# A fixed order table in place of a list scheduler, with convolution taps spread over three engines, in a windowed attention and gated feed-forward kernel

## The chip, the cores and the metric

The kernel runs on one core of one Trainium2 chip. The metric is the device time of one execution in microseconds (us). Executions scatter by one or two per cent, so a kernel is judged by the median of several runs, always beside runs of the kernel before on the same chip. Every ratio here is the mean time of one kernel's fast runs over that of the other kernel's fast runs of the same rounds, so it is not quite the ratio of the medians that are quoted with it. A difference between two variants in us, where it says "by the ratios", is the difference of their two ratios times the median of the kernel before (about 235 us). A run counts as slow when it lies more than 1.5% above the fastest run of its kernel, and as fast otherwise. The *granted clock* is the share of TensorE's full clock that the chip allowed.

Engine names in profile lines: PE is TensorE, PEld its weight loads, DVE is VectorE, ACT is ScalarE, POOL is GpSimd, SPq is the queue of the engine that issues most transfers. A trailing q means an engine's sequencer, and "issue" is time in which nothing that the profile shows was waited for.

## The reference

Attention over a band of 32 positions to each side, then a feed-forward layer with a three-tap convolution along the sequence and a gate:

```python
B, H, S, D = 8, 8, 576, 64          # d_model 512, d_ff 1024
scores = q @ k.T / sqrt(D);  mask = abs(i - j) <= 32
attn   = softmax(where(mask, scores, -1e9)) @ v
x      = attn.transpose(0, 2, 1, 3).reshape(B, S, H * D)
h      = maximum(x @ w_in, 0.0)
conv_out = sum(conv_w[k] * h_padded[:, k:k + S, :] for k in range(3))
gate   = 1.0 / (1.0 + exp(-conv_out))
out    = (h * gate) @ w_out
```

## The kernel before

The sequence of all batches is cut into twelve chunks of 384 positions, numbered 0 to 11. Attention of a pair of batches makes the input of three chunks. A *unit* is one chunk times 128 of the 1024 hidden columns (there are 96, eight of them in two halves). Its convolution runs on TensorE, one matmul with a diagonal matrix for each tap. In most units the middle tap is done by VectorE, which adds `h * w` onto the sum in PSUM:

```python
on_dve = m < P["tap"][c]              # tap: (0, 0, 8, 8, 8, 8, 8, 8, 7, 8, 8, 8)
kks = (0, 2) if on_dve else (0, 1, 2)
def emit_pc(e_):
    for kk in kks:
        tensor.matmul(pc.ap[:, 0:nc_], diag_w[:, kk, m, :], taps(kk), start=(kk == 0), stop=(kk == 2))
...
if on_dve:
    def emit_tap(e_):
        vector.scalar_tensor_tensor(
            out=in3(pc.ap), in0=taps(1), scalar=conv_w_sb[:, 1, m:m + 1], in1=in3(pc.ap),
            op0=ALU.mult, op1=ALU.add)
```

The relu stands on ScalarE, the diagonals, the masks and the "shifts" (copies of v moved by 64 partitions) on VectorE. GpSimd only casts. No order is written down: each operation carries costs, a priority and a list of engines, and a list scheduler simulates the engines and takes the ready operation of lowest priority:

```python
'e_vo': (('DVE',), ('DVE',), ('DVE',)),      # engines for the shifts
'mask': ('DVE',),
...
op(f"pc {u}", {"PE": len(kks) * (nc_ / 2400.0 + 0.0025)}, emit_pc, prio + 0.5, ...)
order = pl.run(P["start"], (0.107, "filler", P["thin"]), P["fill"], pf)
for t, _, e, o in order:
    o.emit(e)                                 # or a filler: a matmul on a tile of zeros
```

The softmax here doesn't subtract the row's maximum and nothing guards it: scores larger than these inputs give would overflow.

Of the kernel before, what the change touches and what calls it, by code (L numbers as in the profile page):

```python
# [9 lines left out]
FP32 = mybir.dt.float32  # L11
# [5 lines left out]
class Pool:  # L17


    def __init__(self, bufs):  # L20
        self.bufs = bufs
        self.free = [(-1.0, i) for i in range(len(bufs))]


    def take(self, span):

        if not self.free:
            return None
        self.free.sort()
        return self.free.pop(0)[1]  # L30

    def room(self, spans, spare):
        return len(self.free) >= len(spans) + spare

    def give(self, now, index, span):
        self.free.append((now, index))

    def ap(self, index, span):
        return self.bufs[index]


class Banks:


    def __init__(self, tile_):
        self.tile = tile_
        self.free = {i: -1.0 for i in range(8)}

    def runs(self, span):
        return [i for i in range(9 - span) if all(i + k in self.free for k in range(span))]  # L50

    def take(self, span):
        if span == 1:
            at = min(self.free, key=lambda i: (i < 3, self.free[i], -i))
        else:
            at = self.runs(span)[0]
        for k in range(span):
            del self.free[at + k]
        return at

    def room(self, spans, spare):
        if len(self.free) < sum(spans) + spare:
            return False
        return all(s == 1 or self.runs(s) for s in spans)

    def give(self, now, index, span):
        for k in range(span):
            self.free[index + k] = now

    def ap(self, index, span):  # L70
        return self.tile[:, 512 * index:512 * (index + span)]


class Slot:


    def __init__(self, pool, span=1):
        self.pool, self.span, self.index, self.users = pool, span, None, 0

    @property  # L80
    def ap(self):
        return self.pool.ap(self.index, self.span)


class Op:
    def __init__(self, name, cost, emit, prio, acquire, spare, mode, two):
        self.name, self.cost, self.emit, self.prio = name, cost, emit, prio
        self.acquire, self.spare, self.mode, self.two = acquire, spare, mode, two
        self.uses, self.after, self.follow, self.left = [], [], [], 0
        self.ready = 0.0  # L90


class Planner:



    LATENCY = {"PE": 0.05, "ACT": 0.045, "DVE": 0.045, "POOL": 0.075, "SP": 0.075}
    switch = 0.1

    def __init__(self):  # L100
        self.ops = []
        self.writer, self.readers = {}, {}
        self.fillers = None

    def op(self, name, cost, emit, prio, reads=(), writes=(), reserve=(), acquire=(), use=(),
           spare=0, mode=None, two=False, behind=None, early=0.0):
        o = Op(name, cost, emit, prio, list(acquire), spare, mode, two)
        o.early = early
        before = set()
        for k in reads:  # L110
            if k in self.writer:
                before |= self.writer[k]
        for k in list(writes) + list(reserve):
            before |= self.readers.get(k, set()) | self.writer.get(k, set())
        for k in reads:
            self.readers.setdefault(k, set()).add(o)
        for k in writes:
            self.writer[k], self.readers[k] = {o}, set()
        before.discard(o)
        o.left = len(before) + (behind is not None)  # L120
        if behind is not None:
            behind.follow.append(o)
        for p in before:
            p.after.append(o)
        o.uses = list(acquire) + [s for s in use if s not in acquire]
        for s in o.uses:
            s.users += 1
        self.ops.append(o)
        return o

    def run(self, start, filler, filler_until, late):

        engines = ("SP", "PE", "POOL", "ACT", "DVE")
        free = dict(start)
        todo = {e: [] for e in engines}
        events, out = [], []
        mode = None
        lock = {"DVE": 0.0, "POOL": 0.0, "PE": 0.0}
        dma_free, rings = 0.0, []
        gone = set()  # L140
        number = {o: i for i, o in enumerate(self.ops)}
        heap, count = [], 0

        def push(t, kind, x):
            nonlocal count
            count += 1
            heapq.heappush(heap, (t, count, kind, x))

        def offer(o):
            for e in o.cost:  # L150
                todo[e].append(o)
                todo[e].sort(key=lambda x: (x.prio, number[x]))


        busy, warm, win = {}, False, -1

        def rate(t):
            nonlocal warm, win
            w = int((t - 1.9) // 3.413)
            while win < w:  # L160
                b = busy.get(win, 0.0) / 3.413
                warm = (b > 0.35) if warm else (b > 0.85)
                win += 1
            return 1.0 if warm else 2.0

        def note(t, d):
            while d > 1e-9:
                w = int((t - 1.9) // 3.413)
                x = min(d, 1.9 + (w + 1) * 3.413 - t)
                busy[w] = busy.get(w, 0.0) + max(x, 1e-6)  # L170
                t, d = t + max(x, 1e-6), d - max(x, 1e-6)

        late.take(1)
        push(filler_until, "free", late)
        for o in self.ops:
            if not o.left:
                push(o.early, "ready", o)
        for e in engines:
            push(free[e], "look", e)
        left = len(self.ops)  # L180
        now = 0.0
        while left or heap:
            if not heap:
                raise RuntimeError("stuck: " + str([(o.name, o.left) for o in self.ops if o not in gone][:40]))
            now, _, kind, x = heapq.heappop(heap)
            batch = [(kind, x)]
            while heap and heap[0][0] <= now + 1e-9:
                _, _, kind, x = heapq.heappop(heap)
                batch.append((kind, x))
            for kind, x in batch:  # L190
                if kind == "ready":
                    offer(x)
                elif kind == "free":
                    x.give(now, 7, 1)
                elif kind == "done":
                    for s in x.uses:
                        s.users -= 1
                        if not s.users:
                            s.pool.give(now, s.index, s.span)
                    for n in x.after:  # L200
                        n.left -= 1
                        if not n.left:
                            push(max(now, n.early), "ready", n)
            if heap and heap[0][0] <= now + 1e-9:
                push(now, "look", None)
                continue
            for e in engines:
                while free[e] <= now + 1e-9:
                    best, blocked = None, False
                    other = {"DVE": "POOL", "POOL": "DVE"}.get(e, "PE")  # L210
                    for o in todo[e]:
                        if o in gone:
                            continue
                        if o.two and lock[other] > now + 1e-9:
                            blocked = True
                            continue
                        need = {}
                        for s in o.acquire:
                            need.setdefault(s.pool, []).append(s.span)
                        if not all(p.room(n, o.spare if p is self.psum else 0) for p, n in need.items()):  # L220
                            continue
                        key = o.prio + (self.switch if e == "PE" and o.mode != mode else 0.0)
                        if best is None or key < best[0]:
                            best = (key, o)
                        if e != "PE":
                            break
                    todo[e] = [o for o in todo[e] if o not in gone]
                    if best is None:
                        if blocked:
                            free[e] = lock[other]  # L230
# [795 lines left out]
```

## Time and profile before

| what | before |
|---|---|
| time, median of 3 runs | 236.68 us (235.42 to 236.8) |
| span of the profiled run | 234.2 us |
| first feed-forward matmul | 24.63 us |
| last matmul of the attention | 187.1 us |
| TensorE's last work | 229.7 us |
| GpSimd | 27% busy, nothing after 158 us |

The three instants in the table cut the span into a ramp, a middle in which attention and feed-forward overlap, and a tail in which only feed-forward is left. The windows view gives for each stretch its length, then the busy time (and number) of PE, PEld, DVE, ACT and POOL, the granted clock of TensorE, the busy share of the DMA engines (which the view can show above 1.00) and GB/s:

```profile
0.00:24.63 24.63, 18.57 (x305) 12.69 (x306) 18.52 (x62) 16.72 (x42) 11.21 (x41) 1.00 0.99 297
24.63:187.10 162.47, 158.69 (x2258) 93.64 (x2257) 149.40 (x346) 139.08 (x335) 51.59 (x61) 1.00 0.82 211
187.10:229.70 42.60, 42.56 (x232) 22.19 (x228) 29.07 (x58) 25.16 (x55) 0.00 (x0) 1.00 0.21 68
```

TensorE fills the tail to the last tenth of a microsecond, VectorE two thirds of it, GpSimd none. The groups to be compared later, with busy time and mean ns of one after the bar:

```profile
L380 DVE SCALAR_TENSOR_TENSOR pf<-hT,conv_w_sb,pf 128x384 f32<-128x384 bf16 x79 | 46.0, 616 | 11.4 <-PE pf L380 10.3 <-ACT attn L380 0.4
L380 PE MATMUL pf<-hT,diag_w 128*128 128x384 bf16 x185 | 40.7, 327 | 0.3 <-DVE diag_w L380 0.2
L380 DVE TENSOR_TENSOR attn<-attn,mask 128x1152 bf16<-128x1152 bf16 x32 | 27.5, 859 | 5.2 <-ACT attn L380 4.8
```

The first is the VectorE tap, the second the tap on TensorE, the third the mask.

### The profile page before, as it was taken

The numbers are of one execution on the slowest core, as the hardware profiler recorded it, in microseconds if no ns is written. First come the engines' busy times: TensorE is split into PE (matmuls) and PEld (weight loads), VectorE is DVE, ScalarE is ACT, GpSimd is POOL, SyncE is SP. The second block draws the span as 40 slices with busy tenths as digits, with TensorE's granted clock in tenths as the row PEclk, the third lists the DMA queues.
The fourth block names the chain that finished last, engine by engine and source line by source line (L and its number), as shares of the span: only waits on it lengthen the run. The fifth ranks groups of instructions, "written<-read, shape, count | busy, mean of one in ns | idle before, by whom it ended". The sixth has DMA issues, their size and how long they took to land.

```text
span 234.2 us, 7175 instructions
## 1 busy us (share of the span) xinstructions
PE 219.8 (94%) x2790; PEld 128.5 (55%) x2790; DVE 197.5 (84%) x463; ACT 181.6 (78%) x432; POOL 62.8 (27%) x101
## 2 busy tenths in 40 slices
PE   7777999899999899999999999999999999999992
PEld 4555556578555555655555555555555655555550
DVE  6489989896999999999999999887997995867271
ACT  3796989999999697798689687797599855766361
POOL 4336655552733531152360210340000000000000
PEclk9999999999999999999999999999999999999999
DMA  6999999999999988649995994981442143211204
GB/s 219 294 261 393 284 264 299 359 201 379 201 321 326 243 273 242 153 55 264 372 196 60 253 186 119 328 219 46 69 75 99 48 88 102 92 45 45 91 3 179
DMA packets 66054, 45.37 MB, mean 194 GB/s; under 512 B 51148, under 2 KB 51172, under 8 KB 66020
## 3 DMA queue, kind: packets, MB, share of 16 engines
q1 hardware_dynamic: 65984, 44.90, 71.1%
q8 instruction: 22, 0.36, 0.8%
q14 instruction: 12, 0.10, 0.1%
q10 hardware_dynamic: 36, 0.01, 0.0%
HBM read 32.52 MB, written 9.44 MB: 179 GB/s over the span
## 4 chain that ended last, share of the span: by engine, by line
PE 65%; DVE 19%; ACT 5%; DMA 3%; issue 3%; SPq 1%; ACTq 0%; POOL 0%; DVEq 0%; POOLq 0%
PE pf L380 65%; DVE gT L380 5%; DVE attn L380 4%; DMA vst<-in_v_dram 3%; DVE pf L380 3%; DVE diag_w L380 3%; ACT attn L380 2%; DVE vo L380 2%; DVE xn L380 1%; SPq L380 1%; ACT pf L380 1%; ACT xn L380 1%; DVE rec L380 1%; DVE qkT L380 1%; DVE xT L380 1%
## 5 line engine op out<-in xcount | busy, mean ns | idle before, releaser
L380 PE MATMUL pf<-xT,w_in_sb 128*128 128x385 bf16 (+2 forms) x416 | 73.9, 315 | 1.4 <-DVE gT L380 0.9
L380 PE MATMUL pf<-w_out_sb,gT 128*128 128x512 bf16 x288 | 67.8, 379 | 0.1
L380 ACT ACTIVATE pf<-pf 128x384 f32<-128x384 f32 (+1 forms) x104 | 47.0, 478 | 13.1 <-DVE pf L380 12.3
L380 ACT ACTIVATE hT<-pf 128x385 bf16<-128x385 f32 (+2 forms) x104 | 48.1, 501 | 11.3 <-PE pf L380 10.1
L380 DVE SCALAR_TENSOR_TENSOR gT<-pf,hT 128x384 bf16<-128x384 f32 (+1 forms) x104 | 51.4, 519 | 5.9 <-ACT pf L380 5.3
L380 DVE SCALAR_TENSOR_TENSOR pf<-hT,conv_w_sb,pf 128x384 f32<-128x384 bf16 x79 | 46.0, 616 | 11.4 <-PE pf L380 10.3
L380 PEld LDWEIGHTS <-w_in_sb 128*128 128x128 bf16 x416 | 38.8, 98 | 24.9 <-issue 2.7
L380 PE MATMUL pf<-hT,diag_w 128*128 128x384 bf16 (+1 forms) x233 | 46.3, 310 | 0.7 <-DVE gT L380 0.3
L380 POOL TENSOR_SCALAR qkb<-st 128x1152 bf16<-128x1152 f32 (+1 forms) x27 | 29.6, 1097 | 57.2 <-DMA st<-in_q_dram 30.5
L380 PEld LDWEIGHTS <-gT 128*128 128x128 bf16 x288 | 27.4, 98 | 29.7 <-ACT attn L380 0.3
L380 ACT ACTIVATE attn<-pf 128x512 bf16<-128x512 f32 (+1 forms) x96 | 41.0, 528 | 2.1 <-PE pf L380 1.9
L380 POOL TENSOR_SCALAR ve<-vst 128x512 bf16<-128x512 f32 x37 | 25.0, 682 | 30.4 <-DMA vst<-in_v_dram 24.6
L380 DVE TENSOR_TENSOR attn<-attn,mask 128x1152 bf16<-128x1152 bf16 x32 | 27.5, 859 | 5.2 <-ACT attn L380 4.8
L380 ACT COPY y<-pf 128x512 f32<-128x512 f32 x32 | 19.5, 612 | 11.1 <-PE pf L380 7.4
L380 PEld LDWEIGHTS <-diag_w 128*128 128x128 bf16 x233 | 19.8, 97 | 13.2 <-issue 0.8
L380 ACT COPY qkT<-pf 128x576 bf16<-128x576 bf16 x36 | 22.7, 660 | 1.8 <-PE pf L380 1.7
L380 DVE TENSOR_TENSOR xn<-pf,rec 128x256 bf16<-128x256 f32 x64 | 23.4, 408 | 0.1
L380 DVE COPY qkT<-pf 128x576 bf16<-128x576 bf16 x28 | 20.4, 748 | 2.9 <-PE pf L380 2.3
L380 DVE COPY vo<-ve 64x520 bf16<-64x520 bf16 (+1 forms) x28 | 15.4, 549 | 2.0 <-POOL ve L380 1.2
L380 PEld LDWEIGHTS <-attn 128*64 128x64 bf16 x576 | 11.8, 110 | 9.4 <-issue 5.7
L380 PE MATMUL pf<-ve,attn 128*64 128x65 bf16 x320 | 15.0, 197 | 2.1 <-DVE attn L380 1.2
L380 PE MATMUL pf<-qkT 64*128 64x64 bf16 x576 | 14.3, 191 | 1.6 <-DVE qkT L380 0.9
(39 smaller groups left out, 139.4 us busy)
## 6 DMA issues: line engine op xcount, KB each, us to landing
st<-in_q_dram SPq DMA_DIRECT2D x16, 576.0 KB, 6.7
st<-in_k_dram SPq DMA_DIRECT2D x16, 576.0 KB, 7.2
out_dram<-y SPq DMA_DIRECT2D x36, 256.0 KB, 2.4
vst<-in_v_dram SPq DMA_DIRECT2D x24, 256.0 KB, 8.5
vst<-in_v_dram SPq DMA_DIRECT2D x16, 192.0 KB, 7.5
st<-in_moe_w_in_dram SPq DMA_DIRECT2D x2, 1024.0 KB, 7.1
st<-in_moe_w_out_dram SPq DMA_DIRECT2D x2, 1024.0 KB, 7.8
xT<-xn SPq DMA_TRANSPOSE x30, 2.5
```

The costliest lines, as they stand in the source:

```text
L380: return lambda *args, **kwargs: fixed(do(*args, **kwargs))
```

## The change

The intent: give GpSimd, idle for most of the span, part of the convolution, so that TensorE has fewer diagonal matmuls; move other work so that no engine is overfull at one time; and write the result down as one searched order instead of leaving it to a greedy list. The core of the diff:

```diff
-class Planner:
-    ... (the list scheduler, its costs, priorities and engine lists)
-P = {'start': ..., 'st': 4, 'attn': 4, 'gT': 2, 'y': 4, ...}
+BUFS = {'st': 3, 'qkb': 5, 'qkT': 3, 'attn': 2, 'rec': 4, 'xn': 3, 'hT0': 8, 'hT1': 6, 'hT2': 6, 'cp': 2, 'gT': 4, 'y': 7}
+CONV = (            # one letter per unit, one row per chunk
+    '33333333',
+    '33q3323r23223321',
+    's222r32q',
... (chunks 3 to 7)
+    'qq23q1q2',
+    'r3rqrq23',
+    '12qrrq1q',
+    '2rrr2rrq',
+)
+ORDER = """
+15D 11D0 12D 1F 17D 2F 13D1 2F 14D 7F 28G 0V 1P0 2F 2V 33V 1F 4G 4F 20G0 21S 2F 16D 5G 1F 22S1 41P120 42P 23S 3G
... (40 more lines: operation number, engine letter, buffers; F is so many fillers)
+    TAPS = {         # taps on TensorE, on GpSimd, on VectorE
+        "3": ((0, 1, 2), (), ()), "2": ((0, 2), (), (1,)), "1": ((0,), (), (1, 2)),
+        "q": ((), (0, 2), (1,)), "r": ((), (0,), (1, 2)), "s": ((0,), (1, 2), ()),
+    }
... (in the unit)
+            def emit_times(e_, cp, kk):
+                gpsimd.tensor_scalar(
+                    out=in3(cp.ap), in0=taps(kk), scalar1=w_tap(kk), scalar2=0.0, op0=ALU.mult, op1=ALU.add
+                )
+            def emit_add(e_, cps=cps):
+                gpsimd.tensor_tensor(out=in3(cps[0].ap), in0=in3(cps[0].ap), in1=in3(cps[1].ap), op=ALU.add)
```

Engine letters: P, V, S, G for the four compute engines, D and Q for transfers issued by the sync engine and by ScalarE. A "q" unit has no matmul: GpSimd makes two products and their sum, and VectorE adds its tap and writes PSUM. The order also puts 24 diagonals and 6 masks on GpSimd, 28 relus on VectorE, and 11 of the long shifts on DMA queues.

## The prediction

> **What bounds the kernel now.** I read the busy shares first, then their course over the span, then the chain that ended last, and only then single groups. Columns of the first fence: busy time, share of the span, instructions; then the same in 40 slices.
>
> ```profile
> PE 219.8 (94%) x2790; PEld 128.5 (55%) x2790; DVE 197.5 (84%) x463; ACT 181.6 (78%) x432; POOL 62.8 (27%) x101
> ...
> PE   7777999899999899999999999999999999999992
> ...
> DVE  6489989896999999999999999887997995867271
> ACT  3796989999999697798689687797599855766361
> POOL 4336655552733531152360210340000000000000
> ```
>
> No engine is free all along: TensorE and VectorE are both at nine tenths in the middle, and in the last fifth VectorE and ScalarE fall off while GpSimd does nothing. So the work is badly spread in time, not only over engines. The windows (columns PE, weight loads, VectorE, ScalarE, GpSimd) give sizes: before the first feed-forward matmul, then up to the end of attention, then the tail.
>
> ```profile
> 0.00:24.60 24.60, 18.57 (x305) 12.69 (x306) 18.49 (x62) 16.69 (x42) 11.18 (x41) 1.00 0.99 297
> 24.60:190.00 165.40, 161.59 (x2275) 95.41 (x2275) 152.33 (x355) 139.97 (x337) 51.62 (x61) 1.00 0.81 208
> 190.00:229.70 39.70, 39.66 (x212) 20.42 (x209) 26.17 (x48) 24.30 (x54) 0.00 (x0) 1.00 0.21 70
> ```
>
> VectorE is 26.2 of 39.7 us busy in the tail: 13.5 us that the middle could have used. The chain says which engine sets the end where:
>
> ```profile
> PE 65%; DVE 19%; ACT 5%; DMA 3%; issue 3%; SPq 1%; ACTq 0%; POOL 0%; DVEq 0%; POOLq 0%
> ...
> 24.21 5.16 DVE diag_w L380 x15
> 29.37 0.48 DVE gT L380
> ...
> 161.90 67.35 PE pf L380 x589
> ```
>
> The last 67 us are TensorE alone. VectorE's 19% lies in the ramp and the middle, and 5.16 us of it is the building of diagonals, one block just when the first chunk starts.
>
> The busy time of PE overlaps itself: eight output matmuls of 379 ns each run from 200.80 to 202.53 in the timeline, 0.216 us apart. I therefore use start-to-start spacings: output matmul 0.216, input matmul of 385 columns 0.166, diagonal matmul 0.163 (384) or 0.083 (192), 18 transposes 0.315, 18 scores 0.35, 8 value matmuls 0.157. Times the counts this is 196.5 us of TensorE, without fillers. On VectorE, back to back in the chain, a tap takes 0.53 us and a gate 0.46.
>
> One more thing decides the risk, the same multiplication by the mask, once beside a GpSimd cast and once without:
>
> ```profile
> 74.36 1.47 DVE L380 TENSOR_TENSOR attn<-attn,mask 128x1152 bf16<-128x1152 bf16 x1
> ...
> 89.89 0.74 DVE L380 TENSOR_TENSOR attn<-attn,mask 128x1152 bf16<-128x1152 bf16 x1
> ...
> 74.08 1.15 POOL L380 TENSOR_SCALAR qkb<-st 128x1152 bf16<-128x1152 f32 x1 [1.87 <-DMA st<-in_q_dram]
> ```
>
> It took 0.74 us with GpSimd idle and 1.47 us when a cast had started 0.28 us earlier.
>
> **What the Trainium skill says.** "SBUF — State Buffer", section "Who interferes with whom": GpSimd and VectorE share one port pair; a VectorE instruction with two SBUF inputs waits for a GpSimd one that reads SBUF, and whichever started first keeps the pair for its whole instruction; an instruction with at most one SBUF input and no two-port mode is free of it. The trace agrees (the two masks). "GPSIMD Engine Reference", section "Performance versus the Vector engine": a two-input operation there costs about 2.6 cycles an element, 4497 ns for 2048 floats against 2293 on VectorE. No two-input operation runs on GpSimd in the kernel before, so its trace cannot say. "Perfetto Trace Analysis", section "Optimizing Scalar/DVE Operations", says that offloading between VectorE and GpSimd might not help, for the same port; section "Optimization Strategy", that interleaving regimes with different busiest engines can. The change does both.
>
> **The change part by part.** Counts come from comparing the instruction lists of both kernels per engine.
>
> TensorE: diagonal matmuls of 384 columns go from 185 to 118, of 192 from 48 to 35: 67 x 0.163 + 13 x 0.083 = 12.0 us less. Four more transposes of xn cost 0.3. Need: 196.5 to 184.8 us.
>
> VectorE loses 24 diagonals (x 0.24 = 5.8), 12 long and 6 short value shifts, most of them now DMAs (12 x 0.70 + 6 x 0.29 = 10.1), 26 taps onto PSUM (13.8), 6 masks (6 x 0.73 = 4.4), 16 normalisations (x 0.33 = 5.3): 39.4 us. It gains 33 long and 2 short taps that add a GpSimd product (18.1 at the price of a tap, an estimate), 8 short taps (2.6), 4 sums (2.0), 28 relus (23 x 0.47 + 5 x 0.27 = 12.2, priced by the slope of the xT casts), 7 copies of qkT (4.6), 10 casts (3.5), 2 copies of y (1.2): 44.2. Net +5 us: VectorE is not relieved at all, it is only filled more evenly.
>
> ScalarE: 28 relus fewer (-10.7), 7 qkT and 2 y copies fewer (-4.9); 64 more normalising activations (64 x 0.22 = 14.1), 9 casts of v (4.7), a few other casts (4.2). Net +7 us.
>
> GpSimd: casts of 128x512 at 0.62 and 128x1152 at 1.15 give 0.83 ns an element plus 0.2. So 60 products of 384 at 0.51 and 3 short ones (31.7), 24 diagonals at 0.30 (7.2), 7 shifts (5.7); by the skill's two-input rate 24 sums at about 1.0 (24) and 6 masks at 2.7 (16), both estimates; fewer casts -16. Net +69: 62.8 becomes about 130 us.
>
> To see what this does to the end I cut each order at the first matmul group of each of the twelve chunks and summed each engine's spacings in each piece; the largest sum is the least that piece can take. After the ramp these largest sums add up to 195.2 us before and 184.4 after. In reality those pieces of the kernel before took 229.7 - 24.6 = 205.1 us, 9.9 more than the sum. The gain lies at the end: pieces 8 to 11 need 61.9 us of TensorE against 45.0 of VectorE before, 55.9 against 52.8 after. Attention is not moved much later; it is taps that leave TensorE in the chunks where VectorE and GpSimd were idle.
>
> Sum: ramp 24.6 + 184.4 + the same loss 9.9 + 4.5 from TensorE's end to the end of the span + 2.5 by which the timed 236.68 exceeds the span of 234.2 = 225.9 us. Three corrections. The ramp: first FFN still needs all of batch 0, VectorE loses the diagonals and its shifts, but ScalarE's work before that point grows from 17.1 to 19.3 and a v load goes ahead of the first q; I take -2. The port: +4 (next part). A fixed order for all engines, evidently searched for, should lose less than a greedy list: -4. I predict 224 us, 5% less.
>
> **The rivals.** First, VectorE becomes the bound through the shared port. Masks (26), the 35 taps with two SBUF inputs, casts and shifts on VectorE are some 80 instructions that can be held. GpSimd would be busy 57% of the time with operations of 0.5 to 2.7 us, whose mean remainder I work out as 0.49 us: 80 x 0.57 x 0.49 = 22 us, of which the 32 masks before already paid about 4 (mean 859 ns, free 730). If all 18 us lay on the path the time would be 238 us, no gain. For it: the two masks above, and VectorE's 98% in the windows of the middle. Against it: in the pieces after the ramp TensorE and ScalarE are as large as VectorE, so much of a wait is taken up, and the old scheduler already kept such operations apart, so the new order surely does.
>
> Second, TensorE's relief is fully used and the order is nearly free of waits: ramp 22 + 184.4 + 3 + 7 = 216 us. For it: the 67 us tail shows TensorE can run without a gap when fed. Against it: three engines within 3 us of each other in sum (184.8, 187, 185) cannot all be without gaps in fixed order.
>
> Third, data: staging buffers go from 4 to 3, attention buffers from 4 to 2, and some 2.9 MB of shifts join the DMA queues, whose engines show nine tenths in the first 18 slices. If loads arrive later, fixed orders stall everything behind a late cast: 230 us or more. Against it: loads stand at nearly the same place of the order as before, and GpSimd waited 55 us for q and v without harm to TensorE, whose waits for GpSimd's qkb sum to 1.7 us.
>
> **Range and chances.** The rivals give 216, 230 and 238 around 224; the first and third can partly come together with the second's gain. I take 214 to 233 for 8 in 10. The 2% line is 232.0 us, near the upper end. Chances: 0.83 faster, 0.13 within 2%, 0.04 slower.
>
> **What would show it.** In the changed kernel's page: GpSimd near 130 us and busy to the end; VectorE about 200 to 210 us but now over 90% of the span; TensorE's tail no longer one stretch of 67 us in the chain, with VectorE's share of the chain well above 19%. Port waits would show as masks and two-input taps with means far above 0.75 and 0.6 us, and as GpSimd products above 0.51. The prediction is wrong if the first feed-forward matmul comes later than 27 us, if waits for DMA head the list of waits on TensorE or VectorE, or if the two-input operations on GpSimd take much more than 1.0 us and hold back the taps behind them.

## The result, and the profile after

The changed kernel took 228.91 us (median of 4 runs, 227.31 to 230.37) against 236.61 us; the ratio of the fast runs is 0.9683, interval 0.961 to 0.9757. It is faster, by 3.2% instead of the predicted 5.3%. From the page of its profile, the busy line, three of the rows over 40 slices of the span, and the chain that ended last:

```profile
span 225.6 us, 7189 instructions
...
PE 211.5 (94%) x2720; PEld 122.9 (54%) x2720; DVE 197.3 (87%) x467; ACT 187.5 (83%) x474; POOL 137.7 (61%) x203
...
PE   7698899989989999989999998999999999999993
...
DVE  6279869899999979797999788989999999899990
...
POOL 5978654654376937695368736756386735566640
...
PE 41%; DVE 18%; ACT 17%; DMA 13%; issue 5%; SPq 3%; POOL 2%; DVEq 0%; ACTq 0%; POOLq 0%
```

GpSimd now works to the end, VectorE is no longer thin in the last fifth, and TensorE's share of the chain fell by more than a third. Transfers in the chain went from 3% to 13%. The same three stretches as before, cut at the changed kernel's own instants (first feed-forward matmul 25.80, last attention matmul 185.9, TensorE's end 221.7):

```profile
0.00:25.80 25.80, 21.13 (x329) 14.52 (x329) 17.43 (x56) 18.53 (x46) 19.67 (x65) 0.93 0.98 298
25.80:185.90 160.10, 155.05 (x2207) 90.73 (x2208) 147.20 (x346) 143.11 (x367) 99.01 (x113) 1.00 0.94 230
185.90:221.70 35.80, 35.30 (x185) 17.65 (x185) 32.62 (x67) 25.19 (x63) 19.04 (x26) 1.00 0.25 82
```

The ramp became 1.2 us longer, the middle 2.4 us shorter, the tail 6.8 us shorter: of 8.0 us by which TensorE ends earlier, 6.8 come after the attention is over. There TensorE has 47 instructions fewer, GpSimd works 19 us where it did nothing, and VectorE fills 32.6 of 35.8 us. The tail is still TensorE with hardly a gap (0.5 us), only with less to do.

How much of this is the tail's depends on the cut. Of the 47 instructions, 35 are diagonal matmuls (48 before, 13 now; 5.7 us at the prediction's spacing of 0.163), but 12 are input matmuls (84 and 72; 2.0 us) that the new order runs before the attention ends, so the middle became 2.4 us shorter although it took over 2.0 us of work. Cut at the first input matmul of chunk 8 instead (166.89 us before, 160.68 after), the last stretch is only 1.7 us shorter, because more attention and output matmuls are now left for it. The trace alone thus doesn't settle where the gain lies; the experiments must.

The chain of the changed kernel (start, length, what) ends on TensorE too, and names loads and shifts further up:

```profile
83.06 4.46 DMA vo<-ve
...
109.73 8.84 DMA st<-in_k_dram
...
136.25 48.21 PE pf L232 x603
...
194.01 27.28 PE pf L232 x142
```

And the groups, which answer to the three of before:

```profile
L232 POOL TENSOR_SCALAR cp<-hT,conv_w_sb 128x384 f32<-128x384 bf16 x60 | 37.0, 622 | 44.4 <-ACT hT L232 20.2 <-DVE pf L232 17.0 <-DVE hT L232 6.0
L232 DVE SCALAR_TENSOR_TENSOR pf<-hT,conv_w_sb,pf 128x384 f32<-128x384 bf16 x53 | 31.5, 613 | 1.2 <-PE pf L232 1.1
L232 PE MATMUL pf<-hT,diag_w 128*128 128x384 bf16 x118 | 26.5, 327 | 0.3 <-DVE gT L232 0.3
L232 POOL TENSOR_TENSOR cp<-cp,cp 128x384 f32<-128x384 f32 x23 | 23.8, 1034 | 1.5
L232 DVE TENSOR_TENSOR attn<-attn,mask 128x1152 bf16<-128x1152 bf16 x26 | 23.0, 886 | 2.4 <-ACT attn L232 2.3
L232 DVE SCALAR_TENSOR_TENSOR pf<-hT,conv_w_sb,cp 128x384 f32<-128x384 bf16 x33 | 20.4, 630 | 0.0
L232 POOL TENSOR_TENSOR attn<-attn,mask 128x1152 bf16<-128x1152 bf16 x6 | 14.2, 2371 | 8.4 <-ACT attn L232 8.4
```

Compare the second and the sixth: a tap that reads one SBUF operand takes 613 ns, one that reads two takes 630. Had GpSimd's use of the shared port held VectorE back much, the sixth would stand far above the second.

### The profile page after: what moved, and what is told of

Read it like the earlier page. It is cut to its first block, busy times and chain, and to the rows that moved or that the text cites. A ratio compares the mean times of both kernels' runs of the same rounds, so it can differ in the third digit from the quotient of the medians.

```text
span 225.6 us, 7189 instructions
## 1 busy us (share of the span) xinstructions
PE 211.5 (94%) x2720; PEld 122.9 (54%) x2720; DVE 197.3 (87%) x467; ACT 187.5 (83%) x474; POOL 137.7 (61%) x203
## 4 chain that ended last, share of the span: by engine, by line
PE 41%; DVE 18%; ACT 17%; DMA 13%; issue 5%; SPq 3%; POOL 2%; DVEq 0%; ACTq 0%; POOLq 0%
PE pf L232 41%; DMA st<-in_k_dram 7%; ACT attn L232 6%; DVE pf L232 5%; DVE gT L232 4%; SPq L232 3%; DMA out_dram<-y 3%; ACT xn L232 3%; DVE qkT L232 2%; ACT pf L232 2%; DMA vo<-ve 2%; DVE attn L232 2%; DVE xn L232 2%; ACT qkb L232 2%; ACT y L232 1%
## 5 line engine op out<-in xcount | busy, mean ns | idle before, releaser
L232 PE MATMUL pf<-xT,w_in_sb 128*128 128x385 bf16 (+2 forms) x416 | 73.4, 315 | 3.6 <-ACT hT L232 0.9
L232 PE MATMUL pf<-w_out_sb,gT 128*128 128x512 bf16 x288 | 72.2, 380 | 0.0
L232 POOL TENSOR_SCALAR cp<-hT,conv_w_sb 128x384 f32<-128x384 bf16 (+1 forms) x63 | 38.9, 622 | 46.1 <-ACT hT L232 20.2
L232 ACT ACTIVATE pf<-pf 128x384 f32<-128x384 f32 (+1 forms) x104 | 48.2, 477 | 13.1 <-DVE pf L232 11.1
L232 DVE SCALAR_TENSOR_TENSOR gT<-pf,hT 128x384 bf16<-128x384 f32 (+1 forms) x104 | 52.1, 517 | 5.5 <-ACT pf L232 5.1
L232 PEld LDWEIGHTS <-w_in_sb 128*128 128x128 bf16 x416 | 38.6, 98 | 27.8 <-issue 4.5
L232 ACT ACTIVATE attn<-pf 128x512 bf16<-128x512 f32 (+1 forms) x96 | 41.4, 522 | 1.8 <-PE pf L232 1.8
L232 ACT ACTIVATE hT<-pf 128x385 bf16<-128x385 f32 (+2 forms) x76 | 35.4, 487 | 6.0 <-PE pf L232 5.6
L232 PEld LDWEIGHTS <-gT 128*128 128x128 bf16 x288 | 26.0, 98 | 25.7 <-DVE gT L232 0.5
L232 DVE SCALAR_TENSOR_TENSOR pf<-hT,conv_w_sb,pf 128x384 f32<-128x384 bf16 (+1 forms) x61 | 34.7, 586 | 1.2 <-PE pf L232 1.1
L232 PE MATMUL pf<-hT,diag_w 128*128 128x384 bf16 (+1 forms) x153 | 30.9, 309 | 0.9 <-DVE xn L232 0.6
L232 POOL TENSOR_SCALAR qkb<-st 128x1152 bf16<-128x1152 f32 (+1 forms) x23 | 25.7, 1122 | 7.6 <-DMA st<-in_k_dram 3.2
L232 DVE COPY qkT<-pf 128x576 bf16<-128x576 bf16 x35 | 25.6, 750 | 4.9 <-PE pf L232 4.9
L232 POOL TENSOR_TENSOR cp<-cp,cp 128x384 f32<-128x384 f32 (+1 forms) x24 | 24.4, 1016 | 1.6
L232 DVE TENSOR_TENSOR attn<-attn,mask 128x1152 bf16<-128x1152 bf16 x26 | 23.0, 886 | 2.4 <-ACT attn L232 2.3
L232 ACT ACTIVATE xn<-pf,rec 128x64 bf16<-128x64 f32 x96 | 22.0, 360 | 1.5 <-DVE rec L232 1.5
L232 ACT COPY y<-pf 128x512 f32<-128x512 f32 x30 | 18.1, 605 | 3.9 <-PE pf L232 3.7
L232 DVE SCALAR_TENSOR_TENSOR pf<-hT,conv_w_sb,cp 128x384 f32<-128x384 bf16 (+1 forms) x35 | 21.2, 618 | 0.0
L232 POOL TENSOR_TENSOR attn<-attn,mask 128x1152 bf16<-128x1152 bf16 x6 | 14.2, 2371 | 8.4 <-ACT attn L232 8.4
L232 DVE TENSOR_TENSOR xn<-pf,rec 128x256 bf16<-128x256 f32 x48 | 18.9, 410 | 0.0
L232 ACT COPY qkT<-pf 128x576 bf16<-128x576 bf16 x29 | 18.6, 664 | 0.4 <-PE pf L232 0.2
L232 PEld LDWEIGHTS <-diag_w 128*128 128x128 bf16 x153 | 13.3, 97 | 9.8 <-issue 1.3
```

The source lines that it names most:

```text
L232: return lambda *args, **kwargs: fixed(do(*args, **kwargs))
```

## The experiments

Twelve kernels ran, in four batches. The kernel before ran beside them with medians of 235.05, 235.06, 235.79 and 234.42 us. All gave right results. Every ratio is taken against the kernel before in the same batch. They are told here by what they test, not in the order in which they ran.

The theory from the trace: *the gain is the tail's, where TensorE alone sets the pace and taps left it for idle engines; in the middle nothing was relieved, because what VectorE lost was given back to it.* The rivals: the searched order as such brings the gain; data movement or the ramp hold the rest back.

### The changed kernel again

No edit.

> The changed kernel once more, so that the others of this call are compared with it on the same chip. Expected within 0.5% of 228.9 us; its five runs also show whether the spread of 227.3 to 230.4 us goes with the granted clock (0.974 to 0.991), as the theory 'the ramp is partly run at the halved TensorE clock' says, or does not, as the theory 'arbitration between GpSimd and VectorE differs from run to run' says.

Measured: 227.73 us (226.35 to 229.89), ratio 0.9701 (0.9654 to 0.9748). This is the figure with which the variants below are compared. It was taken in one batch; the four batches ran on four chips, and the changed kernel itself was not in the other three.

The spread goes with the granted clock: of the ten runs of this kernel, the four at a mean clock of 0.974 to 0.985 took 228.59 to 230.37 us, the six at 0.989 to 0.996 took 226.35 to 228.99. So a variant whose fast runs had a lower clock looks a little too slow. What lowers the clock was not tested.

### Taps of the last four chunks back on TensorE

```diff
-    'qq23q1q2', 'r3rqrq23', '12qrrq1q', '2rrr2rrq',     # chunks 8 to 11
+    '22232122', '13121223', '12211212', '21112112',
 # in ORDER: the GpSimd products and sums of these units go, one matmul group stands ahead of the VectorE tap
```

> In chunks 8 to 11 alone the 20 units with taps on GpSimd get them back on TensorE (30 diagonal matmuls, 4.9 us of TensorE); everything else, the order too, stays. Theory 'the tail was bound by TensorE': 4 to 5 us slower than the changed kernel, about 233.5 us. Rival 'VectorE and the shared port bind the tail now': unchanged or up to 2 us faster, since VectorE's two-input taps no longer meet GpSimd.

Measured: 234.46 us, ratio 0.9959 (0.993 to 0.9987), 6.1 us slower than the changed kernel by the ratios. Nearly the whole gain is gone, though only 30 of the 41 diagonal matmuls that the change took from these chunks came back (the other 11 taps stay on VectorE). The last row of its chain, TensorE's last stretch:

```profile
193.31 34.07 PE pf L228 x179
```

It stands against `194.01 27.28 PE pf L232 x142` of the changed kernel: 37 more instructions, 6.8 us more. The attention also ended later (its last matmul at 188.7 us instead of 185.9), as chunk 8 begins at 160.5 us, before that; the stretch after it is 3.3 us longer (188.7 to 227.8 us).

### Taps of chunks 1 to 7 back on TensorE

```diff
-    '33q3323r23223321', 's222r32q', '1232s332', '22q22q22', 'q31s2qrq', '33212q2s', 'r2rq312q',
+    # the same rows with q written as 2, r as 1, s as 3 (19 units); ORDER as in the run above
```

> The same for the 19 units of chunks 1 to 7 (about 31 diagonal matmuls, 5.1 us of TensorE more, 2 us of VectorE sums less, GpSimd freed of some 34 us). Theory 'TensorE binds in the middle too': 4 to 5 us slower, 233.5 us. Rival 'VectorE with the shared port binds in the middle': no slower, or up to 3 us faster, 226 to 229 us.

Measured: 231.69 us, ratio 0.9879 (0.9835 to 0.9924), 4.2 us slower by the ratios. TensorE's share of the chain is 63% again. So the taps that left TensorE in the middle are needed in this order. This does not mean that the middle gained 4 us by the change: it gained 2.4 us. That the order was fitted to these taps and spent the room elsewhere is a guess.

### First q and k ahead of v

```diff
-15D 11D0 12D 1F 17D 2F 13D1 2F 14D 7F 28G 0V 1P0 ...      # v, q, k, v, q, k; cast of v first on GpSimd
+11D0 12D 1F 2F 13D1 2F 14D 15D 17D 7F 0V 1P0 ...          # q, k, q, k, v, v; cast of v after that of q
```

> Only the first loads are put back in the order of the kernel before: all q and k of batch 0 ahead of the v loads, with the first v cast and the first value shift moved behind the first q casts. Theory 'late first q and k': the first feed-forward matmul moves from 25.8 us to about 24.5 us and the time falls by 1 to 2 us, to about 227.5. Rival 'the ramp is set by ScalarE's 19 us of work': the first feed-forward matmul stays within 0.4 us of 25.8 and the time stays at 228.9.

Measured: 232.29 us median; no ratio of fast runs, and the profiled run was in the slow state, so the time says little; the one fast run of six took 227.69 us, like the changed kernel. In the trace the second cast of q and the cast of v stood on GpSimd behind twelve diagonals (4.16 us in the chain from 6.94 us), and the first feed-forward matmul came at 27.16 us. The expectation was not borne out; being of a slow run, the trace doesn't show why.

### The ramp, a second attempt

```diff
 # q and k first as above; GpSimd's casts of q and v ahead of the diagonals, four of the eight diagonal groups after the v shifts
 # (30S, 33V and 37V, a cast and two shifts of v, also stand later)
+... 20G0 21S ... 24G2 28G 3G 4G 5G 6G ... 34G 7G 8G 9G 10G ...
```

> The ramp done properly where e1 was not: q and k of batch 0 loaded first, both q casts of GpSimd ahead of all diagonals (in e1 and in the changed kernel 12 diagonals of 4.2 us stand in front of the second), four diagonals only after the value shifts, the casts of v later. Theory 'the ramp waits for the first q and k': first feed-forward matmul at about 24.3 us instead of 25.8, and 1 to 1.5 us of the whole time if the middle doesn't take it back. Rival 'ScalarE sets the ramp': first feed-forward matmul stays at 25.5 to 26 us. If the ramp is shorter and the time not, the middle is set by data that come at their own pace.

Measured: 234.98 us (230.75 to 238.34), ratio 0.9886 (0.9817 to 0.9955): slower by 4.3 us. The first feed-forward matmul came at 30.12 us instead of the expected 24.3, and 4.3 us later than in the changed kernel: as much as the whole loss. The first rows of its chain:

```profile
2.83 8.11 DMA vst<-in_v_dram
11.72 3.11 POOL diag_w L230 x8
15.19 1.65 POOL diag_w L230 x4
...
20.44 3.65 POOL diag_w L230 x9
```

The v load came back as the first wait, as in the kernel before, and behind it the chain of the ramp runs mostly over GpSimd's diagonals. TensorE also ran at half clock from 14.6 to 18.0 and from 24.8 to 31.7 us, so diagonals and clock are not told apart. Both attempts on the ramp missed, and each moved several things at once: they leave open what binds it.

### Diagonals on VectorE again

```diff
-28G ... 4G ... 5G ... 3G ... 8G ... 9G ... 10G ... 6G ... 7G      # 28 is the cast of v and stays
+28G ... 4V ... 5V ... 3V ... 8V ... 9V ... 10V ... 6V ... 7V
```

> The changed kernel with its 24 diagonals on VectorE again, at the same places of the order. If GpSimd's diagonals (8.9 us, ahead of its casts of q and its shifts) hold up the ramp, the first feed-forward matmul comes 0.5 to 1.5 us earlier than 25.8 us and the time is equal or 1 us better. If ScalarE or the loads set the ramp, the first feed-forward matmul stays within 0.4 us and so does the time; if VectorE does, it comes later by up to 2 us.

Measured: 227.42 us, ratio 0.9664 (0.9616 to 0.9712): the same as the changed kernel. The first feed-forward matmul came at 25.68 us against 25.80. That part of the change neither helped nor cost, which is in line with the doubt, quoted in the prediction, about moving work between VectorE and GpSimd.

### Shifts issued from ScalarE's queue

```diff
-... 999D ... 1000D ... 1094D ... 1095D ...     # the 11 long shifts of v that are transfers; four of them shown
+... 999Q ... 1000Q ... 1094Q ... 1095Q ...
```

> The 11 value shifts that are DMAs are issued from ScalarE's queue instead of the one queue of all loads, stores and transposes; nothing else. Theory 'in the middle, small transfers wait behind prefetched q and k loads in the one queue': the DMA share of the chain falls from 13% to below 8% and the time by 1 to 3 us, to ratio 0.957 to 0.965. Rival 'VectorE and ScalarE set the middle, the DMAs in the chain are only the last of several that come together': within 1 us of the changed kernel (ratio 0.97), or slower by what ScalarE pays for issuing.

Measured: 233.34 us, ratio 0.9876 (0.9846 to 0.9907), 4.1 us slower by the ratios. The profiled run was in the slow state and is used for nothing. Eight of its nine fast runs had a granted clock of 0.976 to 0.985, so part of this may be clock. Taking the shifts out of the one queue in this way is no remedy; whether waiting in it costs anything stays open, because ScalarE's cost of issuing was not measured apart.

### Shifts on VectorE again

```diff
-... 999D ... 1000D ... 1094D ... 1095D ...     # all 11
+... 999V ... 1000V ... 1094V ... 1095V ...
```

> The same 11 shifts back on VectorE, as in the kernel before (11 x 0.70 = 7.7 us more of VectorE, 2.9 MB less for the DMA engines). Theory 'queue': faster or equal, ratio 0.96 to 0.97, as the data is there at once and the DMA engines are relieved. Rival 'VectorE sets the middle': 4 to 8 us slower, ratio 0.99 to 1.0.

Measured: 235.36 us, ratio 1.0009 (0.9982 to 1.0035), 7.2 us slower by the ratios, the whole gain. Its busy line, and the window from 125 to 150 us (columns as before):

```profile
PE 211.3 (91%) x2694; PEld 123.7 (53%) x2720; DVE 208.0 (89%) x478; ACT 188.2 (81%) x474; POOL 139.8 (60%) x203
...
125.00:150.00 25.00, 20.96 (x264) 11.50 (x267) 23.11 (x49) 19.38 (x51) 14.37 (x18) 1.00 0.77 205
```

VectorE got 10.7 us more, the DMA engines' share in that window fell to 0.77 (1.13 in the changed kernel), and the kernel became slower all the same. The attention ended at 193.7 us instead of 185.9, and the tail kept its length, so the whole loss lies before the tail: in this order the middle cannot take more VectorE work, and the transfers that the shifts added were worth their price.

### More output buffers

```diff
-BUFS = {... 'gT': 4, 'y': 7}
+BUFS = {... 'gT': 3, 'y': 10}       # used in turn
```

> Ten output buffers instead of seven, paid for with three gT buffers instead of four. The chain of the changed kernel has a store of 6.04 us in the middle, after which ScalarE goes on. Theory 'copies of y wait for the buffer of an old store': 1 to 2 us faster, ratio about 0.962, that store gone from the chain. Rival: no change (ratio 0.97).

Measured: 227.6 us, ratio 0.9688 (0.9636 to 0.9741): no change. The output transfer that the changed kernel's chain shows at 97.46 us (6.04 us) was not what held it. A row in the chain is a candidate, not yet a cause.

### Eleven relus back on ScalarE

```diff
 # relu of chunks 1 to 3, where VectorE has it (11 of 28): engine letter
-... V ...
+... S ...
```

> The changed kernel with 11 of its VectorE relus, those of chunks 1 to 3 (in the stretch 50 to 80 us, where VectorE is 10.0 of every 10 us busy), on ScalarE again; all else, the order too, as it is. About 5 us of VectorE's busy time move to ScalarE, which is about 9 of 10 us busy there. Theory 1, VectorE's own work binds the middle of the changed kernel: giving it less work is worth 1 to 3 us, ratio to the kernel before 0.956 to 0.966 where the changed kernel had 0.970. Theory 2, ScalarE is as tight as VectorE there, so no engine can take the work: no change or up to 4 us slower, ratio 0.968 to 0.985, and ScalarE shows 9.8 or more of 10 us in 50 to 80 us with a larger share of the chain. Theory 3, in a fixed order any move of this kind costs, because the orders were fitted around it: over 4 us slower.

Measured: 228.93 us (228.25 to 231.2), ratio 0.9766 (0.9718 to 0.9815), 1.5 us slower by the ratios, which is hardly clear of the noise (the interval of the changed kernel reaches to 0.9748); a gain of 1 to 3 us is excluded. Two windows, 50 to 80 and 80 to 100 us, of the changed kernel and then of this one:

```profile
50.00:80.00 30.00, 29.13 (x477) 18.29 (x476) 30.00 (x74) 26.19 (x66) 19.10 (x20) 1.00 1.04 269
80.00:100.00 20.00, 18.48 (x260) 10.25 (x259) 17.00 (x42) 17.51 (x42) 14.01 (x13) 1.00 1.09 249
```

```profile
50.00:80.00 30.00, 28.71 (x470) 18.22 (x474) 28.01 (x69) 27.62 (x71) 19.32 (x21) 1.00 1.03 272
80.00:100.00 20.00, 16.43 (x226) 9.60 (x221) 13.34 (x35) 17.15 (x43) 13.22 (x13) 1.00 1.04 255
```

VectorE was 30.00 of 30 us busy and now has 2 us free, yet TensorE did no more. Afterwards all engines were thinner; there the chain of this variant shows a shift and ahead of it a load:

```profile
70.23 10.17 DMA st<-in_k_dram
...
83.65 6.29 DMA vo<-ve
```

The shift landed at 89.9 us, in the changed kernel at 87.5 (83.06 + 4.46). So theory 1 of the expectation falls as it stood: VectorE's fullness is not by itself what limits 50 to 80 us. Theory 2's time came true but its sign did not (ScalarE 27.6 of 30 us, not 9.8 of 10). Late transfers were not among the theories, and that they cost the 1.5 us, if it is real, is argued from this one trace, not shown.

### The kernel before, with the last four chunks' taps laid as in the changed kernel

The list scheduler, its priorities and all else stay:

```diff
+    TAIL = {8: "qq23q1q2", 9: "r3rqrq23", 10: "12qrrq1q", 11: "2rrr2rrq"}
-        on_dve = m < P["tap"][c]
-        kks = (0, 2) if on_dve else (0, 1, 2)
+        kk_pe, kk_pool, kk_dve = TAPS[TAIL[c][m] if c in TAIL else "2" if m < P["tap"][c] else "3"]
 # products and sums on GpSimd as in the changed kernel, two float buffers for them
```

> The kernel before, with its list scheduler, and another part alone: in chunks 8 to 11 the taps lie on TensorE, VectorE and GpSimd as in the changed kernel. Theory 'the tail is bound by TensorE alone': 4 to 6 us faster, ratio 0.975 to 0.983, the whole of it after the last value matmul. Rival 'only the searched order makes the taps pay, a greedy list meets GpSimd's long latency': ratio 0.99 to 1.01.

Measured: 230.68 us (229.03 to 232.7), ratio 0.9772 (0.973 to 0.9815). Its tail, from the last attention matmul to TensorE's end:

```profile
187.10:223.40 36.30, 35.78 (x185) 17.66 (x184) 32.85 (x68) 23.05 (x53) 18.91 (x26) 1.00 0.24 75
```

36.3 us where the kernel before has 42.6 and the changed kernel 35.8. The attention ends at 187.1 us as in the kernel before, so the whole gain lies after it; from the first input matmul of chunk 8 to TensorE's end it is the same (57.6 us against 62.8). Here the place of the gain doesn't hang on the cut. This one part, with the old scheduler, brings 2.3 of the 3.0% that the changed kernel had in its repeat: about three quarters. It does not rest on a fixed order.

### The kernel before, with the long shifts as transfers

```diff
- 'e_vo': (('DVE',), ('DVE',), ('DVE',)),
+ 'e_vo': (('DVE',), ('DVE',), ('SP',)),
```

> The kernel before, with its list scheduler, and one part of the change: the 12 long value shifts of batches 2 to 7 are DMAs instead of VectorE copies (12 x 0.70 = 8.4 us off VectorE). Theory 'VectorE binds the middle', which the return of the shifts in the new order suggests (7 us slower): 3 to 6 us faster than before, ratio 0.975 to 0.987, the gain lying before the last value matmul. Rival 'in the old order TensorE sets the middle, so that relief of VectorE is worth little': ratio 0.99 to 1.0.

Measured: 247.55 us, ratio 1.0514 (1.0462 to 1.0567), 12 us slower. VectorE fell from 84% to 75% of the span and waited for ScalarE instead. First row of its waits (engine and tile, waited for; us in total, times, longest):

```profile
DVE attn L380 <- ACT attn L380: 21.3, 16, 5.3
```

The expectation failed. One engine changed in a list is enough to make the scheduler's order worse by more than the whole change gained; that its priorities had been tuned to the old lists is the likely reason, not tested. So "the same part in the other kernel" is a fair test only where, as in the tail, little hangs on the order.

## Why the prediction was right or wrong

**The direction and the main mechanism were right.** It said that the gain lies at the end, in pieces 8 to 11, by taps that leave TensorE where VectorE and GpSimd were idle, and gave 6.0 us less of TensorE there. The tail became 6.8 us shorter. Undoing these taps loses nearly all of the gain (0.9959), and having them alone gives three quarters of it (0.9772). The 6.0 itself rests on a slip: 55.9 us comes out of the prediction's spacings only if one counts from 163.93 us in the trace, the second group of chunk 8. Its first group stands at 160.68 us among those of chunk 7, and from there TensorE needs 59.1, so by that cut the relief is 2.8 us. Counted by taps alone, chunks 8 to 11 lost 41 diagonal matmuls (65 to 24), 6.7 us.

**The counts of the change held.** TensorE's long diagonal matmuls 118, ScalarE 5.9 us more busy (predicted 7), GpSimd 137.7 us (about 130). VectorE ended level (197.5 to 197.3 us) where 5 us more were predicted, which bears out "not relieved at all". Of GpSimd's prices the sum was right (predicted 1.0, mean 1034 ns), the mask too dear (2.7 against 2371 ns), the product too cheap (0.51 against 622 ns) and the diagonal too (0.30 against 388 ns). Most of the product's excess is not waiting for the port: in the tail of the old-scheduler variant its shortest was 579 ns and its median 586, so the price taken from casts was wrong.

**The sum was 5 us too low; its terms show where.** Measured in the profiled run and its timed median:

| term of the sum | predicted | measured |
|---|---|---|
| ramp, to the first feed-forward matmul | 22.6 | 25.8 |
| largest sums of the pieces after it | 184.4 | (same working) |
| loss beyond them, port +4 and order -4 included | 9.9 | 221.7 - 25.8 - 184.4 = 11.5 |
| from TensorE's end to the end of the span | 4.5 | 225.6 - 221.7 = 3.9 |
| timed median beyond the span | 2.5 | 228.91 - 225.6 = 3.3 |
| sum | 223.9 | 228.9 |

The last term is no property of the kernel: the profiled run was the fastest of the four (227.31 us, 1.7 beyond its own span).

**The largest error is the ramp: "I take -2".** It became 1.2 us longer, 3.2 us off. The prediction weighed ScalarE's extra work and the v load ahead of q against VectorE's relief and let VectorE win. The chain of the ramp shows the other side:

```profile
1.83 6.50 DMA st<-in_k_dram
...
9.66 2.92 PE pf L232 x51
...
16.40 2.95 ACT attn L232 x7
```

VectorE, which filled this part of the chain before, gave way to the first k load, to TensorE and to ScalarE, 5.00 of 5.00 us busy from 15 to 20 us. Moving the diagonals between GpSimd and VectorE changed nothing here, so that part of VectorE's relief was worth nothing to the ramp; this is shown. The timeline of the kernel before says why little could come of it. The only diagonals that VectorE made before the first feed-forward matmul are these:

```profile
5.15 1.40 DVE L380 TENSOR_SCALAR diag_w<-ident,conv_w_sb 128x128 bf16<-128x128 bf16 x6
```

They took 1.4 us, and until 12.2 us VectorE then waited three times for others (0.49, 1.82 and 1.18 us). The other 18 came from 24.1 us on, when the ramp was all but over: the prediction named the diagonals as a relief of the ramp. That ScalarE or the loads bind it is argued from the chain; the two attempts to use it failed.

One more thing differs: TensorE's granted clock from 10 to 15 us was 1.00 before and 0.69 after (0.66 to 0.80 in the other fast profiles that keep the ramp's order). In the changed kernel it was 0.50 for 3.4 us from 9.7 us, which is the TensorE row of the chain above. No run tests this by an edit, but the record speaks against a large cost: two variants as fast as the changed kernel (diagonals on VectorE, more output buffers) had three runs at a mean clock of 1.00, in which such a stretch has no room (3.4 us at half clock take 0.008 off the mean). They took 226.66, 227.48 and 227.54 us, the five runs at 0.989 to 0.992 took 226.75 to 227.81.

**The two corrections after it, +4 for the port and -4 for the order, nearly cancelled as predicted but not for the reasons given.** The port's cost on VectorE stayed where it was: masks 26 x (886 - 730) ns = 4.1 us, as before (32 x (859 - 730) ns = 4.1), and two-operand taps 33 x (630 - 613) ns = 0.6 us. So the first rival's 18 us of new waits did not appear, and +4 was too much. But the order did not save 4 either: the loss grew to 11.5 us. That the two together came out near zero, as predicted, is luck. By TensorE's own need, the middle's work fell by 4.6 us (148.6 to 144.0, from the spacings that the prediction used) and its length by 2.4. The relief that the middle received was about half lost.

**What holds the middle is only partly settled.** More VectorE work in it costs 7.2 us, so VectorE has no room. Less VectorE work, with the order as it is, gains nothing. Issuing the shifts from ScalarE's queue or having more output buffers gains nothing either. Three engines near their sums, and DMA engines near full share up to 150 us, leave no single culprit. The third rival (late data) cannot be ruled out: transfers went from 3% to 13% of the chain, and the eleven-relu run lost its time beside a late shift. Three staging buffers instead of four were not tested, and stay open. (The prediction saw the DMA engines of the kernel before at nine tenths in the first 18 slices; slices 15 to 18 of its page read 8, 8, 6 and 4.)

**Signs that failed.** VectorE was expected over 90% of the span and well above 19% of the chain; it has 87% and 18%. None of the three signs of being wrong came: 25.8 us is under 27, no wait for a DMA heads the list of TensorE or VectorE, and the sums took 1.03 us. The 67 us stretch of TensorE did break up, as predicted, but into 48 and 27 us rather than into VectorE's.

**The parts do not add up, and should not be added.** Undone one at a time in the fixed order, the tail's taps cost 6.1 us, the middle's 4.2 and the shifts 7.2, together 17.5, where the whole change brought 7.0 in the same comparison (0.9701). A searched order is fitted around all its parts: taking one out shows that the order leans on it, not what it would bring alone.

No variant beat the changed kernel clearly; the ones with the diagonals on VectorE and with more output buffers equal it.

## What to carry to other kernels

Look for the stretch in which one engine is full and another idle, and price the move there: four chunks of convolution taps, moved in a tail that TensorE alone set, brought most of what a rewrite of the whole schedule brought. In a stretch where three engines are all near full, moves may mostly change which of them is named: here about half of the arithmetic came. Undoing a part of a fixed order overstates the part; adding it alone to the old kernel is the better test, but only if the old schedule does not fall apart over it.

## What the Trainium skill lacked or had wrong

- "SBUF — State Buffer", section "Who interferes with whom": the rule holds nothing on how often the lock bites, and the 22 us of waiting that the prediction worked out from it was far too much. With GpSimd busy for 61% of the span, VectorE taps with two SBUF inputs took 630 ns in the mean against 613 with one, and the masks 886 against 859 before, where GpSimd was busy 27%. No run shows the rule itself to be wrong.
- "GPSIMD Engine Reference", section "Performance versus the Vector engine": it prices a two-input operation on floats, and the float sum agrees with the 1.0 us estimated from it (1034 ns for 384 elements). It has no figure for two bf16 inputs, which are cheaper (2371 ns for 1152 elements, 2.7 us estimated), and none for a product of bf16 by a per-partition factor into floats (586 ns in the median for 384 elements, more than casts had led me to expect).
